# Half-height strip tasks, and the last FFN block in two parts with its weights loaded once, in a two-layer segment-recurrent transformer kernel

## The chip, the cores and the metric

One core of a Trainium2 chip runs the whole kernel. The metric is device time in microseconds (us), the median of several runs. TensorE is called PE below, VectorE DVE, ScalarE ACT, GpSimd POOL, and SyncE SP.

## The reference

The input x is 2048 tokens of 512 numbers, bf16. Two layers follow, each of an attention part A and a feed-forward part B, with the same weights in both layers:

```
x = x + A(layernorm(x));  x = x + B(layernorm(x));  x = x + A(layernorm(x));  x = x + B(layernorm(x))
```

A goes through 64 segments of 32 tokens, one after the other, since each needs the memory that the one before it wrote:

```
for s in range(64):                          # H = 32 heads of 128, 8 memory rows
    h = concat([mem, xs])                    # 8 + 32 rows of 512
    q, k, v = h Wq, h Wk, h Wv               # 32 heads x 128
    p = softmax(mask(q k^T / sqrt(128)))     # 40 x 40 for each head
    o = (p v) Wo                             # 40 rows of 512
    mem = o[:8];  out[s] = o[8:]
```

B is token by token: `h = sigmoid(x w_gate) * (x w_up)` with 1792 columns, then `h w_down`.

## The kernel before, in words

**Steps.** The first layer's segment t and the second layer's segment t - 6 are worked on in one step t (`emit_step`, L633), so there are 70 steps. With both layers the moving operand has 80 columns (40 for each), in steps 0 to 5 and 64 to 69, with one layer, 40. For six heads at a time a step makes q and k (L704, Wq and Wk stationary), copies them from the PSUM bank (L952, the line of all such copies), makes scores (L718), a softmax on DVE and ACT (L731 to L763), the transpose of the probabilities (L777), probabilities times V (PV, L788) and the product with Wo (L805), which is summed over all heads in one bank. At its end the memory rows go to the next step's hT (L818, both layers; L823, one) and the outputs to `oxT` (L830).

**V.** The x rows of V are made ahead of time for whole blocks (`v_pass`, L558; matmuls on L568, 512 columns), go to a scratch in DRAM (`scr`) and come back in time into the five `vsb` buffers (L665). The memory rows, and eight x rows, can only be made in the step itself: this is the strip (L670 to L687). Its 32 matmuls have 32 stationary columns each, four of them beside one another in the four column strips of the array; they write two banks, which are copied to `sst`, from where four DMAs on SP's queue (L685) bring them to vsb. All strips read all of `wv_sb`, the V weights. PV of the same step reads vsb.

**FFN.** When four segments of a layer are done, a block of 128 tokens, `ffn` (L832) transposes oxT (L843), adds x (L849), normalizes (`layernorm_T`, L516: statistics on DVE, a power on POOL at L526, the scaling on ACT at L529, a transpose on PE at L538), and runs seven pairs of gate and up tiles (L869, 16 matmuls a pair), tanh on ACT (L874), a product on DVE (L876), and 14 down matmuls (L888) into one bank. L897 adds x. The gate, up and down weights don't fit beside the attention weights: each `ffn` loads them anew in 21 loads of 256 KB, issued by POOL (L861, L862, L883), into rings of three buffers each (`wg`, `wu`, `wd`). The last FFN, block 15 of layer two, needs the last step's output, so that it begins when all steps are done. Its output goes out by SP (L909) from the one buffer `xo`.

**What sets the order.** Nothing is run in the order of this text. Each piece is a task with an engine, a duration that the author wrote down (`mm_ns`, `dve_ns`, `act_ns`), a latency, and keys that it reads and writes. The `Planner` (L82) lays the tasks on the engines: `forward` (L202) takes the task with the largest tail of work behind it among those that are ready and whose buffers are free; `backward` (L165) makes new tails from the plan; `plan` (L132) repeats both for ten rounds and keeps the round with the least planned span. PSUM banks are a pool of eight; FFN and layer norm tasks ("bg") may hold three. The instructions are then issued in the planned order, each engine's own in sequence, with semaphores from the data.

**Start.** The weights are loaded by SP (`load_weights`, L469) while V of twelve blocks is made (`v_group`) with the FFN's rings as buffers.

Of the kernel before, what the change touches and what calls it, by code (L numbers as in the profile page):

```python
# [81 lines left out]
class Planner:  # L82
# [48 lines left out]

    def plan(self, rounds=10):  # L132

# [203 lines left out]
class Kern:  # L337
# [131 lines left out]
    def load_weights(self):  # L469
        nc, pl = self.nc, self.pl  # L470
        wq_v = self.Wq.rearrange("(c p) h e -> p c (h e)", p=P)
        wk_v = self.Wk.rearrange("(c p) h e -> p c (h e)", p=P)
        wv_v = self.Wv.rearrange("(c p) h e -> p c (h e)", p=P)
        wo_v = self.Wo.rearrange("h e d -> e h d")

        def ld(dst, src, ns, keys):
            pl.add("SP", ns, lambda: nc.sync.dma_start(out=dst, in_=src), w=keys, boost=self.boot())

        xb = list(self.boot_x)
        for h0 in range(0, self.H, 8):  # L480
            cs = slice(h0 * P, (h0 + 8) * P)
            ld(self.wv[:, :, cs], wv_v[:, :, cs], P * self.DC * 8 * P * 2 / 300.0, [("wv", h) for h in range(h0, h0 + 8)])
            for b in xb[:3]:
                self.load_x(b, *self.boot_x[b])
            xb = xb[3:]
        for g, (h0, gsz, us) in enumerate(self.groups):
            cs = slice(h0 * P, (h0 + gsz) * P)
            nb = P * self.DC * gsz * P * 2
            for nm, sb, v in (("wq", self.wq, wq_v), ("wk", self.wk, wk_v)):
                ld(sb[:, :, cs], v[:, :, cs], nb / 200.0, [(nm, h) for h in range(h0, h0 + gsz)])  # L490
            ld(self.wo[:, h0:h0 + gsz, :], wo_v[:, h0:h0 + gsz, :], P * gsz * self.D * 2 / 200.0, [("wo", h) for h in range(h0, h0 + gsz)])
# [23 lines left out]

    def layernorm_T(self, xb, xkey):  # L516
        xkeys = xkey if isinstance(xkey, list) else [xkey]
# [4 lines left out]
        xn = pl.buf(self.xnp)  # L522
        pl.add("DVE", dve_ns(D), lambda: nc.vector.bn_stats(out=ln[:, 0:6], in_=xb), r=xkeys, w=[lk])
        pl.add("DVE", 100, lambda: nc.vector.bn_aggr(out=ln[:, 6:8], in_=ln[:, 0:6]), r=[lk], w=[lk])
        pl.add("DVE", 80, lambda: nc.vector.tensor_scalar(out=ln[:, 8:9], in0=ln[:, 7:8], scalar1=EPS, scalar2=None, op0=ALU.add), r=[lk], w=[lk])  # L525
        pl.add("POOL", 640, lambda: nc.gpsimd.tensor_tensor(out=ln[:, 9:10], in0=ln[:, 8:9], in1=self.negh[:], op=ALU.pow), r=[lk], w=[lk])  # L526
        pl.add("DVE", 80, lambda: nc.vector.scalar_tensor_tensor(out=ln[:, 10:11], in0=ln[:, 6:7], scalar=-1.0, in1=ln[:, 9:10],
                                                                  op0=ALU.mult, op1=ALU.mult), r=[lk], w=[lk])
        pl.add("ACT", act_ns(D) + 294, lambda: nc.scalar.activation(out=xn[:, :], in_=xb, func=ACTF.Identity, bias=ln[:, 10:11], scale=ln[:, 9:10]),  # L529
               r=xkeys + [lk], w=[xn])  # L530
# [5 lines left out]
        def tr():  # L536
            for c in range(DC):
                nc.tensor.transpose(out=pst()[:, c, :], in_=xn[:, c * P:(c + 1) * P], identity=self.ident[:])  # L538

        pl.add("PE", DC * mm_ns(P), tr, r=[xn], w=[B])  # L540
        return pst, B
# [91 lines left out]
    def emit_step(self, t):  # L633
# [35 lines left out]

        def strips():  # L670
            for q in range(2):
                for c in range(DC):
                    for i in range(4):
                        k = 2 * i + q
                        nc.tensor.matmul(vb[q][32 * i:32 * i + 32, :], lhsT=hT[:, c, SCOL:SCOL + 32], rhs=self.wv[:, c, k * 512:(k + 1) * 512],  # L675
                                         start=(c == 0), stop=(c == DC - 1), skip_group_check=True)

        def add_strips():
            sb = pl.buf(self.sstp)
            pl.add("PE", 2 * DC * (mm_ns(512) + 12) + 150, strips, r=hkeys + [("wv", h) for h in range(H)], w=vb, use=[sb])  # L680
            for q in range(2):
# [149 lines left out]

    def ffn(self, j, b):  # L832
        nc, pl = self.nc, self.pl
        D, DC, FC = self.D, self.DC, self.FC
        ox = self.oxT[j][b % 2]
        OB = pl.buf(self.bank, "bg")
# [4 lines left out]
        def tr():  # L841
            for c in range(DC):
                nc.tensor.transpose(out=pso()[:, c * P:(c + 1) * P], in_=ox[:, c, :], identity=self.ident[:])  # L843

        pl.add("PE", DC * mm_ns(P), tr, r=[("oxT", j, b % 2, q) for q in range(BLK)], w=[OB])
        si = self.xw.pop((j, b))
        xi = self.nxt("xa", len(self.xa))
        xa = self.xa[xi]
        pl.add("DVE", 335, lambda: nc.vector.tensor_tensor(out=xa[:], in0=pso(), in1=self.xs[si][:], op=ALU.add),  # L849
               r=[OB, ("xs", si)], w=[("xa", xi)])  # L850
        ti = self.nxt("xnT", len(self.xnT))
        xnT = self.xnT[ti]
        pst, B = self.layernorm_T(xa[:], ("xa", xi))
        pl.add(("ACT", "DVE"), copy_ns(D, True), lambda: (xnT[:], pst()), r=[B], w=[("xnT", ti)])
        hi = self.nxt("hff", len(self.hff))
        hff = self.hff[hi]
        for jp in range(FC // 2):
            gi = self.nxt("wg", self.NG)
            wg, wu = self.wg[gi], self.wu[gi]
            fs = slice(jp * 2 * P, (jp + 1) * 2 * P)  # L860
            pl.add("POOL", 760, lambda wg=wg, fs=fs: nc.gpsimd.dma_start(out=wg[:], in_=self.wgv[:, :, fs]), r=[("wo", self.H - 1)], w=[("wg", gi)] + (["boot"] if self.cnt["wg"] <= self.NG else []), lat=4000.0)  # L861
            pl.add("POOL", 760, lambda wu=wu, fs=fs: nc.gpsimd.dma_start(out=wu[:], in_=self.wuv[:, :, fs]), r=[("wo", self.H - 1)], w=[("wu", gi)] + (["boot"] if self.cnt["wg"] <= self.NG else []), lat=4000.0)  # L862
            GB = pl.buf(self.bank, "bg")
            for i in range(2):
                def mm(i=i, wg=wg, wu=wu, GB=GB):
                    gu = GB[:, :].rearrange("p (a n) -> p a n", a=4)
                    for k, W in ((0, wg), (1, wu)):
                        for c in range(DC):
                            nc.tensor.matmul(gu[:, 2 * i + k, :], lhsT=W[:, c, i * P:(i + 1) * P], rhs=xnT[:, c, :],  # L869
                                             start=(c == 0), stop=(c == DC - 1))  # L870
                pl.add("PE", 2 * DC * mm_ns(P), mm, r=[("xnT", ti), ("wg", gi), ("wu", gi)], w=[GB])
            hi2 = self.nxt("th", 2)
            th = self.th[hi2]
            pl.add("ACT", act_ns(2 * P, True), lambda th=th, GB=GB: nc.scalar.activation(out=th[:], in_=fview(GB[:, 0:1], [(2 * P, 2), (1, P)]), func=ACTF.Tanh, scale=0.5),  # L874
                   r=[GB], w=[("th", hi2)])
            pl.add("DVE", dve_ns(2 * P, True), lambda th=th, GB=GB, jp=jp: nc.vector.scalar_tensor_tensor(  # L876
                out=hff[:, 2 * jp:2 * jp + 2, :], in0=th[:], scalar=1.0, in1=fview(GB[:, P:P + 1], [(2 * P, 2), (1, P)]), op0=ALU.add, op1=ALU.mult),
                r=[GB, ("th", hi2)], w=[("hff", hi, jp)])
        DB = pl.buf(self.bank, "bg")
        for ip in range(FC // 2):  # L880
            di = self.nxt("wd", self.ND)
            wd = self.wd[di]
            pl.add("POOL", 760, lambda wd=wd, ip=ip: nc.gpsimd.dma_start(out=wd[:], in_=self.wdv[:, 2 * ip:2 * ip + 2, :]), w=[("wd", di)] + (["boot"] if self.cnt["wd"] <= self.ND else []), lat=4000.0)  # L883

            def dm(ip=ip, wd=wd):
                for k in range(2):
                    i = 2 * ip + k
                    nc.tensor.matmul(DB[:, 0:D], lhsT=hff[:, i, :], rhs=wd[:, k, :], start=(i == 0), stop=(i == FC - 1))  # L888
            pl.add("PE", 2 * mm_ns(512), dm, r=[("hff", hi, ip), ("wd", di)], w=[DB])
        if j == 0:  # L890
# [3 lines left out]
        else:  # L894
            oi = self.nxt("xo", len(self.xo))
            xo, ok = self.xo[oi], ("xo", oi)
        pl.add("DVE", dve_ns(D, True), lambda: nc.vector.scalar_tensor_tensor(out=xo[:], in0=DB[:, 0:D], scalar=0.5, in1=xa[:], op0=ALU.mult, op1=ALU.add),  # L897
               r=[DB, ("xa", xi)], w=[ok])
# [9 lines left out]
        else:  # L908
            pl.add("SP", 430, lambda: nc.sync.dma_start(out=self.out[b * P:(b + 1) * P, :], in_=xo[:]), r=[ok])  # L909

    def trace(self):
        self.fill = {}
        self.load_mem0()
        p0 = self.pre1(0)
# [10 lines left out]
        for t in range(self.NSTEPS):  # L925
# [8 lines left out]
            s = t - self.LAG  # L934
            if s >= 0 and s % BLK == BLK - 1:
                self.ffn(1, s // BLK)
# [75 lines left out]
```

## Time and profile before

| | |
|---|---|
| median of 6 runs | 1908.57 us (1905.95 to 1915.85) |
| the profiled execution | 1910.33 us, its span 1908.6 us |
| PE busy | 1848.3 us, 97% of the span |
| DVE, ACT, POOL busy | 1286.7, 1184.0, 590.0 us |
| mean granted PE clock | 0.99 |
| q and k (L704), 17920 matmuls | 30% of the chain that ended last |
| Wo (L805), gate and up (L869), V (L568) | 14%, 10%, 8% of that chain |
| strips (L675), down (L888) | 6%, 5% of that chain |
| FFN weight loads | 224 for each of wg, wu, wd, 256 KB each, some 4.1 to 4.7 us from issue to landing |

The span is the time from the first to the last instruction on the chip. Busy time of PE is modelled from the starts of its matmuls. The chain is followed back from the last instruction: at each step to what released it, or to the instruction before it on its engine.

### The profile page before, as it was taken

The page shows a single profiled execution, that of the slowest core. Times are in us where ns is not written, and L with a number is a line of the kernel's source. Part 1 is how long each engine was busy: PE and PEld are TensorE (multiplying, and loading weights), DVE is VectorE, ACT ScalarE, POOL GpSimd, SP SyncE. Part 2 cuts the span into 40 slices and gives each one's busy share as a digit, 9 for nine tenths or more (in the row PEclk, how much of TensorE's full clock was granted, in tenths as well). Part 3 has the DMA queues.
Part 4 walks back from the last instruction along what each step waited for, and adds up shares of the span by engine and source line. Part 5 has one row for each costly group of instructions (what it writes and reads, how often), then busy time and mean ns, then how long its engine had stood idle before and what let it go on. Part 6 is the DMA issues. An engine that isn't in the chain of part 4 may idle for free.

```text
span 1908.6 us, 94174 instructions
## 1 busy us (share of the span) xinstructions
PE 1848.3 (97%) x41116; PEld 1586.4 (83%) x41116; DVE 1286.7 (67%) x4213; ACT 1184.0 (62%) x2701; POOL 590.0 (31%) x840
## 2 busy tenths in 40 slices
PE   7989999999999999999999999999999999999997
PEld 3578788988888898979888888988888888988785
DVE  5355677766776667757767777766777666776563
ACT  5655566666666666656666756666666666666553
POOL 6512103332414232332413242332424142323323
PEclk9989999999999999999999999999999999999998
DMA  9733314464635454454636354554636354554534
GB/s 348 248 86 86 107 49 140 132 177 126 179 99 169 118 156 139 141 156 123 183 85 175 115 164 136 143 162 123 184 104 174 106 156 129 148 150 131 162 88 139
DMA packets 130127, 273.82 MB, mean 143 GB/s; under 512 B 29562, under 2 KB 61058, under 8 KB 129714
## 3 DMA queue, kind: packets, MB, share of 16 engines
q0 software_dynamic: 60608, 185.48, 33.0%
q1 hardware_dynamic: 69106, 82.32, 14.8%
q8 instruction: 322, 5.28, 1.2%
q14 instruction: 91, 0.75, 0.1%
HBM read 222.04 MB, written 27.26 MB: 131 GB/s over the span
## 4 chain that ended last, share of the span: by engine, by line
PE 86%; DVE 3%; issue 3%; ACT 3%; DMA 3%; POOL 1%; SPq 0%; ACTq 0%; POOLq 0%; DVEq 0%
PE bank L704 30%; PE bank L805 14%; PE bank L869 10%; PE bank L568 8%; PE bank L675 6%; PE bank L718 5%; PE bank L888 5%; PE bank L788 3%; PE bank L777 3%; DMA vsb<-sst 1%; ACT otsb L952 1%; PE bank L538 1%; DMA wu<-in_B_w_up_dram 1%; DVE st L731 1%; DVE pb L760 0%
## 5 line engine op out<-in xcount | busy, mean ns | idle before, releaser
L704 PE MATMUL bank<-hT,wq_sb 128*128 128x80 bf16 (+1 forms) x8960 | 626.6, 198 | 8.6 <-DVE hT L818 7.1
L704 PE MATMUL bank<-hT,wk_sb 128*128 128x80 bf16 (+1 forms) x8960 | 625.3, 198 | 2.6 <-issue 2.6
L952 ACT CAST qku<-bank 128x480 bf16<-128x480 f32 (+3 forms) x770 | 395.8, 514 | 272.1 <-PE bank L704 250.8
L704 PEld LDWEIGHTS <-wq_sb 128*128 128x128 bf16 x8960 | 459.8, 100 | 30.9 <-issue 12.1
L704 PEld LDWEIGHTS <-wk_sb 128*128 128x128 bf16 x8960 | 452.2, 99 | 2.2 <-issue 2.2
L731 DVE TENSOR_TENSOR st<-bank,maskb 80x240 f32<-80x240 f32 (+1 forms) x732 | 269.8, 369 | 214.9 <-PE bank L718 208.3
L805 PE MATMUL bank<-otsb,wo_sb 128*128 128x80 bf16 (+1 forms) x8960 | 376.8, 198 | 8.3 <-ACT otsb L952 7.0
L805 PEld LDWEIGHTS <-wo_sb 128*128 128x128 bf16 x8960 | 343.5, 99 | 24.6 <-issue 11.9
L861 POOL DMA_DIRECT2D wg<-in_B_w_gate_dram x224 | 170.0, 759 | 352.0 <-PE bank L869 327.3
L883 POOL DMA_DIRECT2D wd<-in_B_w_down_dram x224 | 159.6, 714 | 347.7 <-PE bank L788 128.6
L952 ACT CAST otsb<-bank 128x480 bf16<-128x480 f32 (+3 forms) x420 | 198.3, 485 | 77.5 <-PE bank L788 62.8
L526 POOL TENSOR_TENSOR lns<-lns,negh 128x1 f32<-128x1 f32 x78 | 46.1, 592 | 570.9 <-DVE lns L525 382.0
L760 DVE TENSOR_TENSOR pb<-st,rz 80x480 bf16<-80x480 f32 x348 | 206.6, 594 | 4.8
L741 ACT ACTIVATE st<-st 80x240 f32<-80x240 f32 (+3 forms) x420 | 160.4, 382 | 72.7 <-DVE st L738 70.5
L743 DVE TENSOR_REDUCE sm<-st 80x6 f32<-80x240 f32 (+3 forms) x420 | 152.5, 364 | 72.5 <-ACT st L741 69.2
L952 ACT CAST ptsb<-bank 128x480 bf16<-128x480 f32 (+3 forms) x305 | 150.5, 504 | 45.0 <-PE bank L777 43.2
L718 PE MATMUL bank<-qku 128*80 128x80 bf16 (+1 forms) x2240 | 176.9, 203 | 0.3 <-ACT qku L952 0.3
L869 PE MATMUL bank<-xnT,wg 128*128 128x128 bf16 x1792 | 175.5, 221 | 1.1 <-ACT xnT L952 1.1
L869 PE MATMUL bank<-xnT,wu 128*128 128x128 bf16 x1792 | 175.0, 221 | 1.7 <-DMA wu<-in_B_w_up_dram 1.7
L862 POOL DMA_DIRECT2D wu<-in_B_w_up_dram x224 | 168.2, 751 | 3.5 <-issue 1.1
L718 PEld LDWEIGHTS <-qku 128*80 128x80 bf16 (+1 forms) x2240 | 129.5, 117 | 44.4 <-issue 19.5
L738 DVE TENSOR_TENSOR st<-st,mx 80x240 f32<-80x240 f32 (+3 forms) x420 | 156.2, 372 | 4.3
(94 smaller groups left out, 2533.0 us busy)
## 6 DMA issues: line engine op xcount, KB each, us to landing
wg<-in_B_w_gate_dram POOLq DMA_DIRECT2D x224, 256.0 KB, 4.1
wu<-in_B_w_up_dram POOLq DMA_DIRECT2D x224, 256.0 KB, 4.6
wd<-in_B_w_down_dram POOLq DMA_DIRECT2D x224, 256.0 KB, 4.7
vsb<-scr SPq DMA_DIRECT2D x512, 48.0 KB
vsb<-sst SPq DMA_DIRECT2D x280, 64.0 KB
scr<-vst SPq DMA_DIRECT2D x128, 96.0 KB
wv_sb<-in_A_Wv_dram SPq DMA_DIRECT2D x4, 1024.0 KB
wq_sb<-in_A_Wq_dram SPq DMA_DIRECT2D x5, 768.0 KB
```

What stands on the lines that cost most here:

```text
L704: nc.tensor.matmul(o_ap, lhsT=W[:, c, h * P:(h + 1) * P], rhs=mv(c), start=(c == 0), stop=(c == DC - 1))
L718: nc.tensor.matmul(s_all(SB)[pr, uh - h0 + i, :], lhsT=qku[:, i, 0, 0:ncol], rhs=qku[:, i, 1, 0:ncol], start=True, stop=True)
L731: pl.add("DVE", dve_ns(n, True), lambda gsz=gsz, hs=hs, st=st, SB=SB, pj_=pj_, npj_=npj_, mk=mk, idx=idx: nc.vector.tensor_tensor(out=st[p ...
L738: pl.add("DVE", dve_ns(n), lambda gsz=gsz, hs=hs, st=st, mx=mx: nc.vector.tensor_tensor(out=st[pr, hs], in0=st[pr, hs], in1=mx[pr, hs].uns ...
L741: pl.add("ACT", act_ns(n), lambda hs=hs, st=st: nc.scalar.activation(out=st[pr, hs], in_=st[pr, hs], func=ACTF.Exp, scale=self.scale), r=s ...
L760: nc.vector.tensor_tensor(out=o, in0=st[pr, hs].unsqueeze(1).to_broadcast([npart, 2, gsz, L]), in1=rz[pr, :, 0:gsz].unsqueeze(3).to_broadc ...
L805: nc.tensor.matmul(WB[:, c * ncol:(c + 1) * ncol], lhsT=self.wo[:, h, c * P:(c + 1) * P], rhs=otsb[:, hl, 0:ncol], start=(h == 0 and c == ...
L861: pl.add("POOL", 760, lambda wg=wg, fs=fs: nc.gpsimd.dma_start(out=wg[:], in_=self.wgv[:, :, fs]), r=[("wo", self.H - 1)], w=[("wg", gi)] ...
L862: pl.add("POOL", 760, lambda wu=wu, fs=fs: nc.gpsimd.dma_start(out=wu[:], in_=self.wuv[:, :, fs]), r=[("wo", self.H - 1)], w=[("wu", gi)] ...
L869: nc.tensor.matmul(gu[:, 2 * i + k, :], lhsT=W[:, c, i * P:(i + 1) * P], rhs=xnT[:, c, :], start=(c == 0), stop=(c == DC - 1))
L883: pl.add("POOL", 760, lambda wd=wd, ip=ip: nc.gpsimd.dma_start(out=wd[:], in_=self.wdv[:, 2 * ip:2 * ip + 2, :]), w=[("wd", di)] + (["boot ...
L952: nc.scalar.copy(out=dst, in_=src)
```

## The change

The strip task is cut in two tasks of 16 matmuls, one for each of its two banks, which the planner may place apart. The planner's rounds go from 10 to 24, and the loads of Wq and Wk are planned at 260 bytes per ns instead of 200.

The last FFN (layer two, block 15) becomes two calls: one of 96 tokens, which needs segments 60 to 62, and one of 32 tokens, which needs segment 63. Both use the same weights, which are loaded once (`last_weights`): pairs 0 to 2 go into the rings of three, pairs 3 to 6, 12 loads, into the first three quarters of `wv_sb`, after the last strips have read it. These 21 loads may be issued by SP or by POOL, as the planner chooses. In the order as built SP issues 11 of them and POOL 10. The other FFNs are as before but for names. The partial calls work on the rows (`rw`) and columns of their tokens; the down matmuls write `DB[rw]`, 96 or 32 rows.

```diff
-    def plan(self, rounds=10):
+    def plan(self, rounds=24):
...
-                ld(sb[:, :, cs], v[:, :, cs], nb / 200.0, [(nm, h) for h in range(h0, h0 + gsz)])
+                ld(sb[:, :, cs], v[:, :, cs], nb / 260.0, [(nm, h) for h in range(h0, h0 + gsz)])
...
-        def strips():
-            for q in range(2):
-                for c in range(DC):
-                    for i in range(4):
-                        k = 2 * i + q
-                        nc.tensor.matmul(vb[q][32 * i:32 * i + 32, :], lhsT=hT[:, c, SCOL:SCOL + 32], rhs=self.wv[:, c, k * 512:(k + 1) * 512],
-                                         start=(c == 0), stop=(c == DC - 1), skip_group_check=True)
+        def strips(q):
+            for c in range(DC):
+                for i in range(4):
+                    k = 2 * i + q
+                    nc.tensor.matmul(vb[q][32 * i:32 * i + 32, :], lhsT=hT[:, c, SCOL:SCOL + 32], rhs=self.wv[:, c, k * 512:(k + 1) * 512],
+                                     start=(c == 0), stop=(c == DC - 1), skip_group_check=True)
...
-            pl.add("PE", 2 * DC * (mm_ns(512) + 12) + 150, strips, r=hkeys + [("wv", h) for h in range(H)], w=vb, use=[sb])
+            for q in range(2):
+                pl.add("PE", DC * (mm_ns(512) + 12) + 75, lambda q=q: strips(q), r=hkeys + [("wv", h) for h in range(H)], w=[vb[q]], use=[sb])
...
+    def last_weights(self):
+
+        if self.lw is None:
+            nc, pl = self.nc, self.pl
+            self.lw, k = [], 0
+            flat = fview(self.wv[:, 0, 0:1], [(1, self.DC * self.H * P)])
+            for jp in range(self.FC // 2):
+                row = []
+                for nm, ring, n in (("wg", self.wg, self.NG), ("wu", self.wu, self.NG), ("wd", self.wd, self.ND)):
+                    if jp < n:
+                        i = jp % n
+                        tl, keys, own = ring[i], [(nm, i)], (nm, i)
+                    else:
+                        tl = flat[:, k * 1024:(k + 1) * 1024]
+                        tl = tl.rearrange("p (c f) -> p c f", c=self.DC if nm != "wd" else 2)
+                        h0 = 8 * k % self.H
+                        keys, own = [("wv", h) for h in range(h0, h0 + 8)], ("lw", k)
+                        keys = keys + [own]
+                        k += 1
+                    src = self.wdv[:, 2 * jp:2 * jp + 2, :] if nm == "wd" else (self.wgv if nm == "wg" else self.wuv)[:, :, jp * 2 * P:(jp + 1) * 2 * P]
+                    pl.add(("SP", "POOL"), {"SP": 450, "POOL": 760}, lambda tl=tl, src=src: ("dma", tl[:, :, :], src), w=keys, lat=4000.0)
+                    row.append((tl, own))
+                self.lw.append(row)
+        return self.lw
+
-    def ffn(self, j, b):
+    def ffn(self, j, b, q0=0, nq=BLK):
...
+        last = nq < BLK
+        rw = slice(q0 * SEG, (q0 + nq) * SEG)
+        n = nq * SEG
+        more = last and q0 > 0
...
-        pl.add("PE", DC * mm_ns(P), tr, r=[("oxT", j, b % 2, q) for q in range(BLK)], w=[OB])
+        pl.add("PE", DC * mm_ns(P), tr, r=[("oxT", j, b % 2, q) for q in range(q0, q0 + nq)], w=[OB])
...
+        lw = self.last_weights() if last else None
...
+            if last:
+                (wg, gk), (wu, uk), _ = lw[jp]
...
-                            nc.tensor.matmul(gu[:, 2 * i + k, :], lhsT=W[:, c, i * P:(i + 1) * P], rhs=xnT[:, c, :],
+                            nc.tensor.matmul(gu[:, 2 * i + k, 0:n], lhsT=W[:, c, i * P:(i + 1) * P], rhs=xnT[:, c, rw],
...
+            if last:
+                wd, dk = lw[ip][2]
...
-                    nc.tensor.matmul(DB[:, 0:D], lhsT=hff[:, i, :], rhs=wd[:, k, :], start=(i == 0), stop=(i == FC - 1))
+                    nc.tensor.matmul(DB[rw, 0:D], lhsT=hff[:, i, rw], rhs=wd[:, k, :], start=(i == 0), stop=(i == FC - 1))
...
             s = t - self.LAG
-            if s >= 0 and s % BLK == BLK - 1:
+            if s == self.NSEG - 1:
+                self.ffn(1, s // BLK, 0, BLK - 1)
+                self.ffn(1, s // BLK, BLK - 1, 1)
+            elif s >= 0 and s % BLK == BLK - 1:
                 self.ffn(1, s // BLK)
```

## The prediction

> **What bounds the kernel now.** I read the busy time by stages first, then the chain of waits of the last 90 us, then the chain in the middle.
>
> ```profile
> core 0: us, PE busy (x) PEld busy (x) DVE busy (x) ACT busy (x) POOL busy (x), PEclk, DMA share, GB/s
> 0.00:100.00 100.00, 84.53 (x799) 43.95 (x800) 44.90 (x135) 57.62 (x114) 57.61 (x105) 1.00 0.86 291
> 100.00:350.00 250.00, 237.18 (x5805) 204.97 (x5803) 161.29 (x536) 145.34 (x364) 44.62 (x63) 0.95 0.33 95
> 350.00:1820.00 1470.00, 1450.67 (x32681) 1274.49 (x32678) 1037.49 (x3404) 942.93 (x2112) 462.35 (x638) 1.00 0.50 143
> 1820.00:1881.60 61.60, 60.67 (x1714) 52.15 (x1710) 37.77 (x128) 33.78 (x102) 15.99 (x22) 1.00 0.39 108
> 1881.60:1908.60 27.00, 15.23 (x134) 10.88 (x134) 5.26 (x13) 4.35 (x10) 9.39 (x13) 0.81 0.46 137
> ```
>
> Between 350 and 1881.6 us TensorE (PE) is idle for only 19.3 + 0.9 us: there every added matmul costs its own time. Idle time lies at the start (15.5 us), in the early steps with one layer alone (12.8 us, with the clock at 0.95), and in the last 27.0 us, where 11.8 us are idle and the clock stands at 0.81. That tail is the last block's FFN:
>
> ```profile
> 1881.21 0.37 PE bank L805 x8
> ...
> 1885.73 0.62 PE bank L538 x4
> ...
> 1887.01 4.42 PE bank L869 x40
> ...
> 1894.59 4.92 DMA wu<-in_B_w_up_dram
> ...
> 1905.14 0.69 DVE xo L897
> ```
>
> Call the end of the last Wo matmul (1881.58) T. After it come 5.4 us of transpose, layer norm, transpose and copy up to 1887.01, with PE almost still; then 18.8 us of FFN to 1905.83, among them a load waited for; then 2.8 us for the store of the output. PE has only 112 x 0.056 + 14 x 0.216 = 9.3 us of FFN work there. The clock takes its share:
>
> ```profile
> 1885.00:1891.40 6.40, 5.00 (x45) 4.82 (x46) 0.79 (x2) 2.03 (x4) 2.28 (x3) 0.50 0.16 45
> 1891.40:1898.40 7.00, 4.35 (x46) 2.67 (x44) 0.90 (x3) 0.77 (x2) 6.02 (x9) 0.98 0.85 246
> ```
>
> After the idle stretch the granted clock is 0.50 for 6.4 us, then DMA is busy at 0.85 with the weights.
>
> **The tail, after the change.** In the order as built, of the 96-token part's 112 gate and up matmuls 24 stand before the last Wo matmuls and 88 after them, where they fill the 32-token part's layer norm. Prices: 80 columns take 0.0358 us (72 in 2.58), 128 take 0.056, so 96 take about 0.0424. For 32 columns I take the nearest row:
>
> ```profile
> 1855.00 0.60 PE bank L805 x24
> 19.91 6.91 PE bank L568 x32
> ```
>
> The first is 24 matmuls of 40 columns, 0.025 us each; I take 0.025 for 32 columns too, although 32/40 of it would be 0.020 (0.6 us less in all). The second gives 0.216 for 512 columns, which each down matmul costs whether 128, 96 or 32 tokens are in it. From T: 24 gate/up of 96 columns (1.0), four transposes (0.2), 64 more gate/up (2.7) with 8 down matmuls between (1.7): T + 5.7. The 32-token layer norm meanwhile needs, by the tail's rows, oxT 0.28, transposes, xa 0.42, statistics 0.69 + 0.18 + 0.15, POOL 0.56, 0.16, xn 0.81, with some 0.7 of foreign DVE work between: ready at about T + 5.4, so hidden. Then transposes 0.2, four down matmuls 0.9 (they hide the xnT copy), 112 gate/up of 32 columns 2.8, two last down matmuls of the 96 part 0.4, 14 of the 32 part 3.0: T + 13.0. Output addition 0.7 and store 2.8: T + 16.5, against T + 27.0. **Gain 10.5**. ScalarE and VectorE need some 0.2 and 0.25 us per pair of tiles where PE takes 0.83, so they hide. It rests on the V-space weights being there; below.
>
> **What moves T.** Before T the 96 part adds 24 x 0.0424 and eight transposes: **+1.5**. Nothing pays for it, since PE is busy 41.5 of the last 41.6 us before T. The FFN of block 14, formerly spread up to T, stands almost wholly in the step before, at the same total.
>
> The weights are moved, not added: 21 loads of 256 KB before and after. But 12 of them now go into the V weights and wait for the last step's strips; two of these stand on SP's queue ahead of the four strip copies to vsb, two go out from POOL at the same time. Behind the copies on PE stands everything, for the first probability-times-V (PV) matmuls of that step come, by the order, 3.7 us of PE work after the strips. What such a copy takes, alone and beside weight loads:
>
> ```profile
> 330.75 1.99 DMA vsb<-sst
> ...
> 587.25 4.37 DMA vsb<-sst
> ```
>
> Alone: SP's two load issues (0.44 each, the row of the wv loads) pass while the bank is copied (0.7), then issues of 0.58 and 0.62 and a landing of 2.0, so the second copy is there 4.1 us after the strips: a wait of 0.5. Crowded, with issues of 0.83 as in the last step of before and a landing of 4.4, 7.0: a wait of 3.3, and up to 5 if the load issues are stretched as well. The V-space loads are 3.1 MB, 12.8 us at the 246 GB/s above; the first pair is needed 14 us after the strips and the last after 18, so I cost their lateness at nothing, and at up to 3 if that cover is gone. POOL's power for the 96 part stands behind a wd load that waits for block 14's last down matmuls, 3.7 us after the strips; its transposes come after 6.8 us, so it costs up to 1.5, in the same place. Bounds 0.5 and 5; I take **+2**, nearer the uncrowded row, because eight of the twelve are sent only later.
>
> [...]
>
> **Half strips.** Same 32 matmuls per step, now as 16 + 16, in 43 of 70 steps with other work between:
>
> ```profile
> 1014.86 1.84 PE bank L675 x32
> ```
>
> Four column strips run side by side, so 32 matmuls stream for 8 x 0.216 = 1.73; 0.11 is start and end. An extra block costs at most 43 x 0.11 = 4.7, at least 0; three staggered starts of 0.025 give 43 x 0.075: **+3.2**.
>
> The copies to vsb need both halves. Counting PE work from the second half to the first PV matmul in the two orders, it falls from 6.9 us on average to 5.2 (most of the middle 3.5 to 5). In the trace of before PV follows after 3.8 to 9.0 us; at 3.9 it did not wait, at 4.9 to 5.3, beside weight loads, it did in some steps, by 0.2 to 0.66. SP's issues are stretched, the sign of crowding, in about 22 of 70 steps. Some 17 crowded steps with under 5 us left, 0.3 each beyond today's 1.7: **+3**; bounds -1.7 (all waits gone) and +15 (0.8 in 17 steps and a little in the others).
>
> **The rest of the order.** The 24 planning rounds and the assumed load speed of wq and wk (260 for 200) add no instruction; they only reorder. In the start, 12 of 288 boot V matmuls move from step 0 behind it, into gaps of step 1: 12 x 0.216 = 2.6, and half the early stall at 105.73 (2.0) may go: **-4**; bounds -13 (all idle time of 100 to 350) and +3 (one more wait like the 2.98 of scr<-wu there). In the middle I see two waits that the order touches:
>
> ```profile
> 810.14 3.90 DMA out_dram<-xo
> 814.05 3.72 DMA xo<-in_A_x_dram
> ```
>
> Here x is loaded into the buffer that the output is just leaving; the statistics now stand 11 DVE instructions behind the output addition for 8: 3 x 0.4 us earned. The other, scr<-vst 3.32 and vsb<-scr 1.84 at 975 to 981, has more of its V pass in the earlier step (24 or 28 of 32 matmuls for 20 or 24): **-2** in all; bounds -8 and +5 (one more such wait).
>
> **Sum:** -10.5 + 1.5 + 2 + 3.2 + 3 - 4 - 2 = -6.8. The profiled execution took 1910.33 (span 1908.6), so 1903.5; it stands 1.8 above the median of the six runs, 1908.57. On the median: **1902**. Its own range is 1896 to 1908.
>
> **Rivals.**
> Late weights (0.20): V-space loads crowd the strip copies. Wait 5 for 2, weights late 3, and 7 us at half clock, at which 24 q/k matmuls of 40 columns took 0.91 for 0.70 (126.17 us), so 2: the tail nets -10.5 + 1.5 + 10 = +1, and the rest +0.2: 1910. For it: four 256 KB loads beside the copies. Against: DMA stood at a share of 0.46 over the last 40 us, and most of the loads come later.
> Strips too late for PV (0.10), the slower side: in the middle steps PV catches up with the copies. If half of some 55 steps with under 5.2 us left lose 0.8 each, that is 22 for 3: 1902 + 19 = 1921. It decides above 15.5 us in all, 0.28 for each of 55 steps. For it: the shorter distance in nearly every step. Against: at 3.9 today's steps do not wait.
> A better order (0.15): half the idle time of 100 to 1820 (32 us) goes, and no PV waits: -16 for -6, 0 for +3: 1889. For it: the idle time is there. Against: much of it is DMA that is no quicker afterwards.
> That the 96 tokens run early is itself hardly so, 24 of 112 matmuls; the forecast counts it.
>
> **How the numbers follow.** Forecast 0.55. A run of this kernel tells about 0.3% from no change, 5.7 us: faster is under 1902.8. The forecast is 1 us inside, so of its 0.55 I count 0.36 as faster and 0.19 as same; of late weights 0.02 and 0.18; the better order all faster; the last all slower. That gives 0.53, 0.37, 0.10. The range 1892 to 1911 takes in the forecast, the late weights and the nearer part of the better order.
>
> **What would show it.** Right: from the last Wo matmul to the end 16 to 18 us at clock 1.00, no load in the chain after T; a PV wait of 1 to 3 us on vsb<-sst in the last step; strip blocks of 16 at 0.95 rather than 0.92; waits of PV on vsb<-sst some 5 us in total. Wrong: loads from the weights in the last chain, a clock of 0.50 after T, PV waits above 10 us, or early steps as long as before.

## The result and the profile after

The kernel after takes 1904.8 us (1900.19 to 1910.37), the kernel before 1909.3 us (1904.54 to 1916.24) in the runs beside it: a ratio of 0.9972 [0.9964, 0.9979], or 5.3 us less (4.0 to 6.9; the two medians alone lie 4.5 apart). The interval does not reach 1, so the kernel is faster, but by 0.28%, just inside the 0.3% that the prediction took as the bound of no change. The profiled execution of after took 1906.38 us, its span 1904.6 us: 4.0 below the span of before.

The first view is again the busy time by stages, of after. Its columns are those of the same view of before: the stretch, its length, then the busy time of each engine.

```profile
core 0: us, PE busy (x) PEld busy (x) DVE busy (x) ACT busy (x) POOL busy (x), PEclk, DMA share, GB/s
0.00:100.00 100.00, 86.04 (x962) 47.18 (x963) 46.64 (x145) 56.99 (x115) 52.02 (x96) 1.00 0.86 287
100.00:350.00 250.00, 236.09 (x5718) 200.12 (x5715) 161.61 (x536) 150.17 (x372) 46.69 (x65) 0.98 0.34 96
350.00:1820.00 1470.00, 1451.33 (x32561) 1265.36 (x32559) 1031.83 (x3385) 946.18 (x2116) 465.12 (x639) 1.00 0.50 143
```

The first 100 us hold more matmuls than before (962 for 799), and the clock of the next 250 is 0.98 for 0.95. The middle is as full as it was (1451.33 busy for 1450.67). The second view is the same kind of table around the last step of after. T, the end of the last Wo matmul, is now 1886.78; before it was 1881.58.

```profile
1875.77:1877.98 2.21, 0.16 (x4) 0.06 (x3) 2.14 (x9) 0.25 (x2) 1.79 (x3) 0.90 1.05 242
1877.98:1884.20 6.22, 5.22 (x132) 4.81 (x133) 2.51 (x12) 2.97 (x8) 1.81 (x3) 0.50 1.09 314
1884.20:1886.78 2.58, 2.58 (x80) 2.47 (x77) 0.45 (x2) 1.14 (x4) 0.00 (x0) 0.97 0.57 174
1886.78:1901.80 15.02, 14.27 (x236) 9.59 (x233) 6.52 (x20) 4.78 (x16) 0.57 (x1) 1.00 0.04 10
1901.80:1904.60 2.80, 0.00 (x0) 0.00 (x0) 0.00 (x0) 0.00 (x0) 0.00 (x0) 1.00 0.05 12
```

After T, PE is busy for 14.27 of 15.02 us at clock 1.00, with DMA almost still: the tail is no longer a wait. The loss stands ahead of T. For 2.21 us PE does next to nothing (0.16 us) while DMA is full, and the clock is 0.50 for the 6.22 us that follow. The chain that ended last, of after (start, duration, work), says what PE stood for:

```profile
1847.95 1.84 PE bank L674 x32
...
1868.50 0.98 PE bank L674 x16
...
1872.29 0.48 ACT sst L996
...
1872.78 0.52 SPq L685
...
1873.35 6.03 DMA vsb<-sst
...
1879.43 0.31 PE bank L788 x4
...
1879.74 0.80 PE bank L805 x24
...
1886.58 0.20 PE bank L805 x8
1886.78 1.03 PE bank L904 x24
1887.80 0.33 PE bank L872 x4
1888.13 0.79 PE bank L904 x16
```

The strip copy to vsb takes 6.03 us to land, and PV (L788) stands behind it. No load is in the chain after T. The timelines of after show PE's two waits there (in brackets: the idle time and what ended it) and what SP's queue was sending:

```profile
1877.98 0.45 PE L788 MATMUL bank<-ptsb,vsb 128*128 128x40 bf16 x8 [2.05 <-DMA vsb<-sst]
1879.43 0.31 PE L788 MATMUL bank<-ptsb,vsb 128*128 128x40 bf16 x4 [1.00 <-DMA vsb<-sst]
```

```profile
1871.35 0.37 SPq L992 DMA_DIRECT2D wv_sb<-in_B_w_down_dram  x1
1871.81 0.60 SPq L992 DMA_DIRECT2D wv_sb<-in_B_w_gate_dram  x1
1872.78 2.42 SPq L685 DMA_DIRECT2D vsb<-sst  x4
```

Two loads of 256 KB into the space of the V weights stand on SP's queue ahead of the four strip copies; POOL sends two more, at 1871.58 and 1872.81. From 1875.30 on both send further ones while the copy is still under way.

T to the end fell from 27.0 to 17.8 us (-9.2). From the last step's first q and k matmul to T it rose from 18.8 to 22.8 (+3.95). The remaining +1.3 of the span had gathered before that step. How it gathered is seen from the time at which each step writes the memory rows for the next (the hT writes of L818 and L823, step 68 the last), less the same of before, in us. The table holds the kernels of the experiments too, which are told below:

```
step            0      4      5      6     11     27     28     60     68   span
after        -5.8  -10.3   -6.3   -2.3   -3.2   -2.9   +2.1   +4.3   +1.3   -4.0
tail_only    +0.8   +1.6   +2.2   +2.2   +1.4   +1.3   +2.4   +2.9   +4.6   -0.1
no_tail      -6.5  -11.8   -8.3   -3.8   -2.2   -0.1   +4.2   +7.7   +8.4   +8.9
loads_behind -5.6  -10.3   -6.9   -4.1   -4.8   -4.1   -0.9   +5.3   +3.8   +4.2
x_buffer     -5.6  -10.6   -7.4   -1.9   -3.0   +1.5   -2.1   +6.4   +5.2   +0.4
split_queues -6.1  -10.9   -8.1   -5.4   -6.1   -5.5   -1.4   +0.2   -2.7  -10.4
down_last    -5.2  -10.8   -8.8   -5.7   -7.1   -6.2   -1.4   +3.0   +3.6   -2.4
whole_strips -7.6  -10.7  -11.7   -8.7   -8.4   -4.5   -3.3   -4.1   -4.7  -10.7
ten_rounds   -5.0   -7.4   -4.4   -0.1   -1.6   +0.9   +3.5   +7.3   +8.9   +3.9
rounds_only  -0.3   -4.7   -6.4   -1.7   -4.7   -2.3   -2.1   -0.3   +0.3   +0.2
whole_200    +0.6   -5.0   -6.1   -1.5   -3.9   -1.7   -0.8   -0.5   -1.4   -7.2
split_whole  -7.4  -10.9  -12.1   -9.2  -11.9   -8.5   -8.4   -6.6   -6.8  -15.7
split_x_whole -7.8 -11.0  -12.0   -9.0  -10.0   -3.6   -8.1   -9.4   -6.4  -15.0
```

After is 10.3 us ahead at step 4, gives 8.0 of it back in steps 5 and 6, and 5.0 in step 28. Such a lead can also be work put off: of the 10.3, 1.8 is work of the first FFN (20 gate and up and 3 down matmuls, 20 x 0.056 + 3 x 0.216) that before does in step 4 and after in step 5. In step 0 the lead of 5.8 holds 15 V matmuls (3.2 us) that after does in step 1.

Steps 1 to 4 of before, of after and of rounds_only (the kernel before with 24 rounds), in the columns of the first view:

```profile
101.68:186.03 84.35, 78.25 (x2134) 68.01 (x2134) 49.00 (x172) 43.99 (x132) 11.90 (x17) 0.86 0.25 69
```

```profile
95.87:175.69 79.82, 75.60 (x2130) 64.47 (x2129) 48.56 (x172) 45.74 (x134) 12.86 (x19) 0.96 0.28 78
```

```profile
101.44:181.30 79.86, 74.63 (x2133) 64.82 (x2133) 48.91 (x172) 43.91 (x132) 11.82 (x17) 0.96 0.26 72
```

After earns 4.5 us there, with less idle time and a clock of 0.96 for 0.86, and rounds_only earns as much.

### The profile page after: what moved, and what is told of

Same layout as the page of the kernel before. It is cut to its first block, busy times and chain, and to the rows that moved or that the text cites. A ratio compares the mean times of both kernels' runs of the same rounds, so it can differ in the third digit from the quotient of the medians.

```text
span 1904.6 us, 94394 instructions
## 1 busy us (share of the span) xinstructions
PE 1851.5 (97%) x41250; PEld 1577.2 (83%) x41250; DVE 1284.5 (67%) x4214; ACT 1193.8 (63%) x2722; POOL 581.4 (31%) x824
## 4 chain that ended last, share of the span: by engine, by line
PE 88%; DMA 4%; DVE 3%; issue 2%; ACT 1%; POOL 1%; SPq 1%; ACTq 0%; POOLq 0%; DVEq 0%
PE bank L704 30%; PE bank L805 15%; PE bank L904 10%; PE bank L568 8%; PE bank L674 7%; PE bank L928 5%; PE bank L718 5%; PE bank L788 4%; PE bank L777 3%; DMA vsb<-sst 2%; PE bank L538 1%; DMA xo<-in_A_x_dram 1%; SPq L685 1%; DVE ptsb L998 0%; DVE st L731 0%
## 5 line engine op out<-in xcount | busy, mean ns | idle before, releaser
L896 POOL DMA_DIRECT2D wg<-in_B_w_gate_dram x217 | 164.7, 759 | 478.8 <-PE bank L904 428.8
L922 POOL DMA_DIRECT2D wd<-in_B_w_down_dram x217 | 154.5, 713 | 222.0 <-PE bank L928 172.6
L526 POOL TENSOR_TENSOR lns<-lns,negh 128x1 f32<-128x1 f32 (+1 forms) x79 | 49.0, 621 | 529.8 <-DVE lns L525 427.4
L904 PE MATMUL bank<-xnT,wu 128*128 128x128 bf16 (+2 forms) x1784 | 171.3, 218 | 1.3 <-DMA wu<-in_B_w_up_dram 1.3
L904 PE MATMUL bank<-xnT,wg 128*128 128x128 bf16 (+2 forms) x1784 | 172.1, 219 | 0.0
L996 ACT CAST ptsb<-bank 128x480 bf16<-128x480 f32 (+3 forms) x277 | 134.6, 495 | 50.1 <-PE bank L777 46.0
L897 POOL DMA_DIRECT2D wu<-in_B_w_up_dram x217 | 163.3, 753 | 5.0 <-PE bank L904 1.6
L788 PE MATMUL bank<-ptsb,vsb 128*128 128x80 bf16 (+1 forms) x2240 | 140.6, 198 | 22.8 <-DVE ptsb L998 9.0
```

The source lines that it names most:

```text
L788: nc.tensor.matmul(OB[:, hl * ncol:(hl + 1) * ncol], lhsT=self.vsb[(4 * t + h // 8) % 5][:, (h % 8) * P:(h % 8 + 1) * P], rhs=ptsb[:, hl, ...
L904: nc.tensor.matmul(gu[:, 2 * i + k, 0:n], lhsT=W[:, c, i * P:(i + 1) * P], rhs=xnT[:, c, rw], start=(c == 0), stop=(c == DC - 1))
L996: nc.scalar.copy(out=dst, in_=src)
```

## The experiments

Each edit is against the kernel after unless it says otherwise. A ratio is to the kernel before, run on the same chip in the same rounds; a difference of two kernels is taken from their ratios, times 1909, with the two half-widths added in squares. One profile can lie far from its kernel's median (no_tail's lies 4.1 us above it, x_buffer's 5.9, the others within 3.3), so the ledger above says where, and the ratio how much.

**tail_only: the divided last FFN alone.** The strips are whole again, the rounds 10, the load speed 200.

```diff
-    def plan(self, rounds=24):
+    def plan(self, rounds=10):
...
-                ld(sb[:, :, cs], v[:, :, cs], nb / 260.0, [(nm, h) for h in range(h0, h0 + gsz)])
+                ld(sb[:, :, cs], v[:, :, cs], nb / 200.0, [(nm, h) for h in range(h0, h0 + gsz)])
...
-            for q in range(2):
-                pl.add("PE", DC * (mm_ns(512) + 12) + 75, lambda q=q: strips(q), r=hkeys + [("wv", h) for h in range(H)], w=[vb[q]], use=[sb])
+            pl.add("PE", 2 * DC * (mm_ns(512) + 12) + 150, strips, r=hkeys + [("wv", h) for h in range(H)], w=vb, use=[sb])
```

> The changed kernel with the strips in one task of 32 matmuls again, ten rounds and 200 for the loads of Wq and Wk: only the divided last FFN is left of the change. By the ledger (T to the end 9 us shorter, the last step 4 us longer, everything before it about level) it is 3 to 6 us below the kernel before, ratio 0.997 to 0.9985, with 24 of the 43 extra strip blocks' cost no part of it. If instead the new order of the rest made the gain, the tail's parts cancel and it is within 1 us of before.

Measured 1907.49 us, 0.9975 [0.9963, 0.9988]: 4.8 us faster than before. In its trace, taken 2.7 us above its median, it takes 41.9 us for 46.7 from step 68 to the end: 4.7 earned there, while step 68 itself ends 4.6 later in this order.

**no_tail: all but the divided FFN.**

```diff
-            if s == self.NSEG - 1:
-                self.ffn(1, s // BLK, 0, BLK - 1)
-                self.ffn(1, s // BLK, BLK - 1, 1)
-            elif s >= 0 and s % BLK == BLK - 1:
+            if s >= 0 and s % BLK == BLK - 1:
```

> The changed kernel with the last FFN whole again, as before: half strips, 24 rounds and 260 alone. By the ledger (step 68 ended 1.3 us later than before) it is 0 to 3 us above the kernel before, and its last 27 us are those of before. If the new order made the gain, it is 4 to 5 us below.

Measured 1915.27 us, 1.0012 [0.9999, 1.0026]. The rest of the change, taken together, brings nothing, and more likely costs 2 us: the 11.8 us of its start are gone by step 27, and step 68 is 8.4 late. Against after, the divided FFN is worth 7.6 us with a half-width of 2.9.

**loads_behind: the V-space loads behind the strip copies on SP.** It takes the crowding away by sending them only once the copies to vsb are there (pairs 3 to 6); the ring loads stay free to go by SP or POOL.

```diff
-                    pl.add(("SP", "POOL"), {"SP": 450, "POOL": 760}, lambda tl=tl, src=src: ("dma", tl[:, :, :], src), w=keys, lat=4000.0)
+                    if jp < n:
+                        pl.add(("SP", "POOL"), {"SP": 450, "POOL": 760}, lambda tl=tl, src=src: ("dma", tl[:, :, :], src), w=keys, lat=4000.0)
+                    else:
+                        pl.add("SP", 450, lambda tl=tl, src=src: nc.sync.dma_start(out=tl[:, :, :], in_=src),
+                               r=[("vs", (4 * (self.NSTEPS - 1) + i) % 5) for i in range(4)], w=keys, lat=4000.0)
```

> The changed kernel, but the 12 loads into the V weights go out from SP alone, behind the last step's four strip copies. If these loads crowd the copies, the PV wait of the last step falls from 3.1 us to under 0.7, the clock stays at 1.00 before T, and the time is 3 to 5 us below the changed kernel (ratio to before about 0.995), with the loads still in time. If the copies are late for another reason (the bank copy, the distance of 3.7 us), the wait stays above 2; if the loads are then late, a wait of the gate and up matmuls on them of 1 to 4 us takes its place.

Measured 1914.45 us, 1.0015 [1.0005, 1.0025]: 8.2 slower than after (half-width 2.4), where a gain had been expected. The PV wait is gone, but another takes its place, in the chain of loads_behind:

```profile
1881.77 0.89 PE bank L805 x32
1882.66 9.64 DMA wu<-in_B_w_up_dram
...
1892.35 3.06 PE bank L908 x36
```

The planner put a ring load, which the first pairs need, on SP behind five of the V-space loads. It was issued at 1882.66 and landed 9.64 us later. The run says nothing against crowding; it shows that a load that is needed early must not stand behind those that are needed late.

**split_queues: the same, with the ring loads on POOL only.** So that nothing that is needed early stands behind the V-space loads.

```diff
                     if jp < n:
-                        pl.add(("SP", "POOL"), {"SP": 450, "POOL": 760}, lambda tl=tl, src=src: ("dma", tl[:, :, :], src), w=keys, lat=4000.0)
+                        pl.add("POOL", 760, lambda tl=tl, src=src: nc.gpsimd.dma_start(out=tl[:, :, :], in_=src), w=keys, lat=4000.0)
```

(This diff is against loads_behind.)

> The changed kernel, but the nine ring loads of the last FFN go out from POOL alone and the twelve into the V weights from SP alone, behind the last strip copies, so that no ring load stands behind them as wu did in the run before this. If the crowding of the copies was the cost of the last step, both waits are gone there (PV on vsb under 0.7 us, gate and up on loads under 1), the clock stays at 1.00, T to the end is 17 to 18 us and the time is 3 to 5 us below the changed kernel, ratio to before about 0.995. If the loads are too late behind the copies, gate and up wait for the V-space weights by 2 us or more and it is level with the changed kernel.

Measured 1902.22 us, 0.9955 [0.9942, 0.9969]: 3.2 faster than after (half-width 2.9). The busy time of split_queues in its last step, and PE's waits from 1860 us on (us in total, times, longest):

```profile
1866.00:1879.20 13.20, 12.83 (x346) 10.67 (x344) 9.92 (x36) 8.24 (x24) 1.99 (x3) 1.00 0.60 169
```

```profile
PE bank L908 <- DMA wv_sb<-in_B_w_up_dram: 0.4, 1, 0.4
PE bank L538 <- ACT xn L529: 0.2, 1, 0.2
PE bank L908 <- issue: 0.2, 1, 0.2
```

PE is busy for 12.83 of 13.20 us at clock 1.00, PV waits for nothing, and the later loads cost 0.4. The order was planned anew, so the distance has to be looked at too. PE comes to the first PV 4.05 us after the strips in after and 4.5 here, and that alone would take only some 0.5 off the wait. In five kernels with two loads ahead of the copies (after, x_buffer, ten_rounds, down_last, whole_strips) the last wait of PV on them ends 6.6 to 7.5 us after the strips, whatever the distance: with 4.05 it waits 3.05 in all, with 6.1 (whole_strips) 0.9. (tail_only has loads ahead too, and a PV wait of 2.1 that the profile puts down to no copy.) With the loads behind the copies, it waits for nothing at 4.5 (here) and at 4.8 (loads_behind). So nearly all of the 3.05 us of waits, and with them the cold clock of after, came of the V-space loads ahead of the copies. From step 68 to the end split_queues takes 39.0 us for after's 41.4, although T to the end, expected at 17 to 18, is 18.8; the other 4.0 us by which its profile is ahead had gathered earlier.

**x_buffer: of the x blocks that are loaded on the way, all but block 6 go into the second buffer, which the output never uses.**

```diff
-            i = self.nxt("xp", 2)
+            i = 0 if b == 6 else 1
```

> The changed kernel, but of the four x blocks that are loaded on the way only the first goes through the output's buffer, the other three through the second one. The step of 35 us (step 28, PV waiting 7.1 us behind a DVE statistic on x, loaded after the output left) falls to about 30, so 4 to 6 us below the changed kernel, ratio about 0.995, if nothing else is late there. If the order is remade and another wait of that size comes up elsewhere, the time is that of the changed kernel.

In after, step 28 lasts 35.3 us (before: 30.2). Its chain shows x loaded into the buffer that the output is leaving, with PV waiting behind the statistics of that x on DVE:

```profile
806.54 3.79 DMA out_dram<-xo
...
810.35 7.10 DMA xo<-in_A_x_dram
...
817.48 0.69 DVE lns L523
818.17 0.23 DVE ptsb L998
```

With the other buffer step 28 takes 26.5 us, but most is given back: step 25 takes 31.0, step 42 32.7, and PV waits for vsb<-sst 13.0 us in all (after: 8.8). Measured 1904.86 us, 0.9963 [0.9949, 0.9978]: 1.7 less than after with a half-width of 3.1, not told apart from nothing.

**down_last: the 32-token part's down matmuls after all its gate and up matmuls.** The same 126 matmuls, with fewer changes between the two kinds.

```diff
-            pl.add("PE", 2 * mm_ns(512), dm, r=[hk, dk], w=[DB])
+            pl.add("PE", 2 * mm_ns(512), dm, r=[hk, dk] + ([("hff", 0, i, "b") for i in range(FC // 2)] if more and ip == 0 else []), w=[DB])
```

> The changed kernel, but the 32-token part's 14 down matmuls (32 stationary columns, one column strip of the array) all stand behind its 112 gate and up matmuls (whole array). If the change between strip and whole array costs some 0.1 us each time, as the two blocks of a strip of 16 show against one of 32 (0.98 twice for 1.84), the 16 gate and up matmuls take 0.40 and the pairs of down matmuls 0.43 instead of 0.50 and 0.54, and T to the end falls from 17.8 to about 16.7 us; in the time about 1 us, which the rounds can hardly tell. If the slow pace has another cause (the weights' place, 32 columns), the rows stay at 0.50 and 0.54.

Measured 1907.89 us, 0.9984 [0.9973, 0.9995]: 2.3 slower than after (half-width 2.5), as step 68 came 3.6 late. But T to the end fell from 17.8 to 16.8. The chains, first of after, then of down_last:

```profile
1896.06 0.50 PE bank L904 x16
1896.55 0.54 PE bank L928 x2
1897.09 0.50 PE bank L904 x16
1897.59 0.54 PE bank L928 x2
```

```profile
1897.04 0.79 PE bank L904 x32
...
1898.30 1.19 PE bank L904 x48
1899.49 3.14 PE bank L928 x14
```

In a row a gate or up matmul of 32 columns costs 0.79 / 32 = 0.0247 us and a down matmul 3.14 / 14 = 0.224. In turns, 16 cost 0.50 for 0.395, and two 0.54 for 0.448: about 0.1 for each change of kind.

**whole_strips: the strips whole, all else as in after.** The diff is the last hunk of tail_only.

> The changed kernel with the strips in one task of 32 again; 24 rounds, 260 and the divided last FFN stay. If half strips cost what their rows show (43 blocks of 0.12 us and 2.4 us more of PV waits), it is 2 to 6 us below the changed kernel, ratio to before 0.994 to 0.996. If half strips earn as much elsewhere (fewer waits, the start), it is level with it, 0.996 to 0.998; if they earn more, above 0.998.

Measured 1897.38 us, 0.9931 [0.9916, 0.9946]: 7.8 faster than after (half-width 3.2). Its lead at step 4 is after's, but it keeps it: step 6 is at -8.7 for -2.3. PV waits on vsb<-sst 5.8 us in all, 0.9 of it in the last step.

**ten_rounds: 10 rounds, all else as in after.** The diff is the first hunk of tail_only.

> The changed kernel with ten planning rounds instead of 24. If the rounds only choose between plans that are alike on the chip, it is within 3 us of the changed kernel, either way (ratio 0.9955 to 0.9985). If the longer search brought part of the gain, it is 3 to 8 us slower.

Measured 1913.0 us, 1.0018 [1.0005, 1.0031]: 8.8 slower than after (half-width 2.9). In the profiles it is 2.9 behind after at step 4, 3.0 at step 60 and 7.6 at step 68; down matmuls wait 6.0 us for DVE in step 28.

**rounds_only: the kernel before, with 24 rounds for 10.**

```diff
-    def plan(self, rounds=10):
+    def plan(self, rounds=24):
```

(This diff is against the kernel before.)

> The kernel before with 24 planning rounds instead of ten, and nothing else. If the longer search earned what the difference of whole strips with and without it says (0.9931 against 0.9975), it is 6 to 10 us below the kernel before, ratio 0.995 to 0.997. If that gain came from 260 for the loads of Wq and Wk, it is within 2 us of before.

Measured 1910.69 us, 0.9998 [0.9987, 1.001]. A gain had been expected, and there is none: of 4.7 us earned by step 4, 1.7 are left after step 6, and at step 60 they are gone.

**whole_200: whole_strips with the load speed of before.** The diff against whole_strips is the middle hunk of tail_only.

> Whole strips, 24 rounds, the divided last FFN, and 200 again for the loads of Wq and Wk. If 260 does nothing by itself, ratio 0.992 to 0.995, as with 260 (0.9931). If 260 made the early start, 4 to 9 us more, 0.995 to 0.998.

Measured 1906.54 us, 0.9979 [0.9965, 0.9992]: 9.2 slower than whole_strips (half-width 3.9; 3.5 between the two profiles), and level with tail_only (0.9975). Its step 0 ends at +0.6, that of whole_strips at -7.6. So it is the load speed, not the rounds, that makes step 0 shorter. The rounds earn something in steps 1 to 4: whole_200 and rounds_only, both with 200, are 5.0 and 4.7 ahead at step 4, and both lose most of it in step 6.

**split_whole: whole_strips with the loads of split_queues.**

> Whole strips, 24 rounds, 260, the divided last FFN, with ring loads from POOL and the V-space loads from SP behind the strip copies. The two gains that the runs showed one by one (whole strips 8 us, the queues 3 us, of which 1 us is left where the wait of the last step is only 0.9) give 1 to 3 us below whole strips alone, ratio 0.9915 to 0.993. If the loads are late behind the copies, it is level or above.

Measured 1896.04 us, 0.9934 [0.9916, 0.9951]: level with whole_strips (half-width 4.4), in which PV had only 0.9 us to lose in the last step. A gain of 1 to 3 us, as expected, could not be told from this.

**split_x_whole: the same, with x_buffer's line.**

> The same with the x blocks in the second buffer. In whole strips alone the output's store and the load of x after it (5.4 and 3.8 us) still stop PE for 4.9 us in step 28. If that wait goes and nothing else comes up, 3 to 5 us below the run beside it, ratio 0.989 to 0.991; if the new order gives it back, as in part it did with half strips, level with it.

Measured 1894.69 us, 0.9907 [0.9891, 0.9923]: the best version, 17.8 us faster than before (14.7 to 20.8), 12.4 faster than after (half-width 3.4) and 5.2 faster than split_whole (4.5). PE's two longest waits of it after the start (us in total, times, longest), whole execution:

```profile
PE bank L788 <- DMA vsb<-sst: 6.2, 15, 1.5
PE bank L805 <- ACT otsb L1000: 6.0, 17, 0.7
```

The last step has no PV wait; q and k wait for the memory rows (L818) 2.2 us for whole_strips' 7.1.

## Why the prediction was right, and where it was not

The forecast was 6.8 us less, the measurement 5.3. Taken in two parts it also stands: the tail with its price before T was put at -10.5 + 1.5 + 2 = -7.0 and measured -7.6 (half-width 2.9, after against no_tail); the rest at +0.2 and measured +2.3 (-0.2 to +5.0, no_tail). For the tail the mechanism was right. That the rest came out near its +0.2 was in good part luck: the start earned 10.3 for 4 and lost 8.0 again, and the middle lost where it was to gain. The steps:

**The tail, -10.5: right in what it does, 1.3 too much.** Clock 1.00, no load in the chain, 17.8 us from T to the end for 16.5. Of the missing 1.3, 1.1 is in the 32-token part. The price of a gate or up matmul was right (0.025 forecast, 0.0247 in a row), but that of the changes was left out: after's last chain has four blocks of 16 and four pairs at some 0.1 more each, 0.8 in all. down_last took most of the changes away and 1.0 went with them. What takes the time in a change the rows do not show. Down matmuls with 32 stationary columns stand there among others with 128; the 96-column part, whose down matmuls have 96, shows nothing of the kind (16 gate and up matmuls take 0.68, 0.0425 each, the 0.0424 of the forecast).

**What moves T, +1.5 and +2: the sum right, its make-up not.** Forecast +3.5, measured +3.95 over the last step. The wait was 3.05, beyond the chosen 2, within the bounds, and near the 3.3 of the crowded sum: crowding was the case, and the choice of +2, nearer the uncrowded row, was wrong. The cold clock was priced only in the rival of late weights, yet it came with a wait of this size. Wo matmuls of that stretch show its price: 24 take 0.80 to 0.91 where they take 0.60 warm, in all some 1.2 us by my count of its rows. Against it stand some 1.9 us of block 14's FFN that have left the step: 1.5 + 3.05 + 1.2 - 1.9 = 3.85. The forecast had counted neither of these two, and it is luck that they nearly cancel. split_queues shows the cause, the loads ahead of the copies. The weights themselves were not late, so that rival was half right: crowding, but no lateness.

**Half strips, +3.2 and +3: size about right, place wrong.** A block of 16 takes 0.98, not 0.95, and one of 32 takes 1.84: 2 x 0.98 - 1.84 = 0.12 a split, 5.2 in 43 steps, more than the 4.7 given as the most. The three starts of 0.025 behind the 3.2 were an estimate of mine that no run shows: in the trace of before the four matmuls beside one another start some 0.003 apart (the strips at 1014.78). What after shows in their place is the 0.12 a split. PV waits on vsb<-sst rose from 3.3 in all to 8.8 - 3.05 = 5.75 outside the last step, by 2.4 for 3; but whole_strips has 4.8 of them too, so only about a microsecond is due to the halving. The halving costs 7.8 (half-width 3.2) by whole_strips, 4.0 (4.2) by split_whole against split_queues, for a forecast of 6.2. The forecast spread it over the middle; the profiles set it into two places. In steps 4 and 5 together after loses 2.8 against whole_strips, and split_queues 2.8 against split_whole; in step 28 it is 3.8 and 4.0. All other steps up to 68 together are 0.7 and 2.8 shorter with the halving, so that the 5.2 of the splits does not show there; what makes up for it is open. Step 6 is mostly not the halving's: it is 2.7 to 5.6 longer than before in all kernels but tail_only, with whole strips too. Waits that after shows in steps 5 and 6 are 1.0 and 2.1 on PV and 2.1 of issue. The 2.1 on PV is put down to a DVE reduction that PV does not read; strip copies had been sent from 222.52 on and PV went on at 225.94, so it was probably theirs. What makes the other is open. The rival that PV would catch up with the copies all through the middle did not come: outside the last step no wait that the profile puts down to them was longer than 1.0.

**The start, -4: the sign right, the size wrong.** The forecast took 12 V matmuls out of step 0 into gaps of step 1, and half of one stall. The move came: 15 of them are done in step 1, whose idle time falls from 3.2 us to 0.1. But at step 4 the lead is 10.3, and it has two sources. One is the load speed: it tells the planner that Wq and Wk arrive sooner, which then puts the q and k of step 0 ahead of V matmuls that were ahead of them. The fourth group of six heads, before and then after:

```profile
73.40 0.26 PE L704 MATMUL bank<-hT,wq_sb 128*128 128x40 bf16 x4
```

```profile
65.77 0.26 PE L704 MATMUL bank<-hT,wq_sb 128*128 128x40 bf16 x4
```

The fifth moves from 85.4 to 75.9, and no q or k matmul of step 0 waits over 0.4 us, so the weights are there. Step 0 ends 5.8 earlier in after, 7.6 in whole_strips, 0.6 later in whole_200. The load speed is worth 9.2 (half-width 3.9) where the strips are whole. The other source is the 4.5 us of steps 1 to 4, which rounds_only has too: shorter waits and, with them, a warmer clock (0.96 for 0.86), which the forecast did not price. "They only reorder" was true of both edits, but the order was worth more than the moved matmuls.

**The middle, -2: wrong.** The wait of step 28 was to be shorter by 1.2 and the step got 5.0 longer. I had counted the DVE instructions behind the output addition, but not how long the x load would take: 7.10 for 3.72. With x loaded as in before, the kernels with half strips lose 2.6 to 5.0 in that step and those with whole strips 0.1 to 1.2, so most of it came with the halving, by way of the order. In after POOL sends three weight loads of 256 KB while x is under way (810.66 to 812.19), and x takes 7.10; in before it sends none in that time, and x takes 3.72. That looks like the crowding of the last step once more.

**Where the gain went.** In the profiles the start earns 10.3 and the tail 9.2. Steps 5 and 6 take back 8.0 (1.8 of it the FFN work that step 4 had put off), step 28 5.0 and the last step 3.95; all other steps together earn 1.4. That leaves 4.0. What stays open: why 24 rounds are worth 8.8 us with half strips and nothing with whole ones (rounds_only, and whole_200 against tail_only). Each change has the whole order planned again, with a fixed latency for every weight load (4000 ns), whatever is sent beside it; that this is why gains are so often given back is only argued here.

## What to carry to other kernels

When new loads are sent as soon as their space is free, look for the small copy on the critical path that is issued at the same moment: put it ahead of them on its queue (behind two of them it took 6.03 us in after; behind the copies, in split_queues, the later loads cost 0.4), and keep loads that are needed early off the queue with the late ones (9.64 us behind five of them in loads_behind). In a kernel that a planner orders, cost an edit of its assumptions by what becomes ready earlier, not by the instructions it adds, and try each part alone, since a part that costs (here the half strips) can hide in a sum that gains. When a kernel seems ahead at some step, count the work done by then: a lead can be work put off. Price narrow matmuls by a run of their own kind and add the changes between kinds (here 0.0247 us for 32 columns, and some 0.1 for a change).

## What the runs showed of the hardware

Near the end of both kernels the clock halved during a short idle time of PE. In after PE did nothing from 1875.9, and by stretches of 0.5 us the clock was 1.00 until 1877.5 and 0.54 from there to 1878.0: some 1.6 us. In before it took from 1882.3 to about 1884.9, 2.6 us, counted from the end of four transposes; from the last Wo matmul ahead of them it is 3.3. It was 0.50 in the 6.22 us from 1877.98 in after and in the 6.40 us from 1885.00 in before, though PE was busy again for 5.22 and 5.00 of them. Not every such idle time did this: in after PE did nothing from 223.83 to 225.94, 2.1 us, and the clock was 1.00 then and up to 240.

A copy of 64 KB (vsb<-sst) landed in 1.99 us with no weight load issued meanwhile and in 4.37 with one of 256 KB issued on POOL's queue meanwhile (before, at 330.75 and 587.25). It took 6.03 in after, behind two loads of 256 KB on its own queue, with two more on POOL's and others sent after it. In loads_behind a load of 256 KB took 9.64 behind five others on SP's queue.
